# Keys of the first four tiles loaded in halves, idle products in any free PSUM bank, and a re-made order, in an attention and two-layer kernel on one core

## The chip, the core and the metric

The kernel runs on one core of a Trainium2 chip. Its engines work side by side, each through its own queue in order: TensorE (PE, with its weight loads, PEld), VectorE (DVE), ScalarE (ACT), GpSimd (POOL), and SyncE (SP), whose queue issues every DMA here. Times are microseconds. The metric is the device time of one launch: 1057.6 us, the median of 3 runs (1056.24 to 1058.17).

## The reference

Four batches of 768 positions with eight heads of 64 go through an attention of a narrow band with a few global keys, then through two feed-forward stages, one after the other:

```
scores = q @ k^T / 8 - slope[h] * dist ;  kept where key < n_global or 0 <= rel < n_local
a = softmax(scores) ;  x = a @ v                    # 3072 tokens x 512
h = x @ w_in  (512 x 2048) ;  x = (h * cos(h)) @ w_out
h = max(x @ w2_in, 0)      ;  out = (h * h) @ w2_out
```

Everything is float32. The kernel carries most numbers as a high and a low float16 part, so that a product becomes three float16 products.

## The kernel before, in words

There are 24 tiles of 128 positions (six in a batch). The first tile of each batch (F0 to F3 here, tiles 0, 6, 12 and 18) sees only its own keys; these four make the first block of 512 tokens, and the other twenty follow in blocks of four. A tile has two head groups of four heads, g0 and g1.

For the four first tiles `attend32` works in float32. `prepare32` loads the keys and queries (`kq`, 512 KB, two of them each 256 KB for tile 0) and the values (`vt`, 256 KB). `group32` then does for one head group: scores (PE L836, 4 matmuls), the bias by products with an identity (PE L918; it needs the tables that ACT writes in L590), the largest (DVE L925), the scaling of that (L908 on POOL or DVE, L906 on ACT), the exponentials with their sums (ACT L932, four of them), a diagonal of the sums' reciprocals (DVE L851, L854, L855), the turning and weighing by that diagonal (PE L866), a copy out of PSUM (`cast`, L538 on ACT or L540 on DVE), the values (PE L875), and the two parts of x (L538 or L540, then DVE L887, into `xy_107`). Tiles after the first of a batch go through `group`: scores L965, reduction L974, exponentials L982, parts `p` (cast L538/L540, low part L525 on DVE or POOL), a transposing DMA (L996), values L1006.

Weights come packed. `decoded` unpacks a pair: DMA `raw` (1 MB, L628), ACT L63, DVE L70; then a cast (L538 or L540) and a low part (L525). The first layer's products are L1149 (first half) and L1165 (second half). The first L1149 that reads all of `xy_107` can start once the last L887 of the four first tiles is done.

The order of all this is made when the kernel is built. Each piece has a due time, shifted by a table (`SHIFTS`, one entry per tile, group or weight), and `Plan.run` puts the pieces on the engines by due time, free buffers and durations that are written in the code; where a piece may run on two engines (a cast on ACT or DVE, a low part on DVE or POOL), `Plan.run` chooses. Every engine then executes its pieces in that order. `idle_products` looks for places where PE has a gap in the plan and puts products with a zero matrix there (L1789, each 128 x 512). SP's DMAs stand on eight semaphores in turn, so that the ninth DMA waits until the first has landed; the buffers named `ld` (nine of them) hold keys, values and weights in turn.

Of the kernel before, what the change touches and what calls it, by code (L numbers as in the profile page):

```python
# [67 lines left out]
def join(nc, f, t, r, n):  # L68
# [14 lines left out]
    ('A', 0, 0): -3.1,  # L83
    ('A', 0, 1): -3.1,
    ('A', 1, 0): -10.1,
# [12 lines left out]
    ('A', 15, 1): -0.3,  # L98
    ('A', 16, 0): 4.6,
    ('A', 2, 0): 0.7,  # L100
    ('A', 2, 1): -3.1,
    ('A', 21, 0): 2.9,
    ('A', 21, 1): -1.8,
    ('A', 23, 1): -6.5,
    ('A', 3, 0): 2.4,
    ('A', 3, 1): -3.1,
    ('A', 4, 1): -0.3,
    ('A', 5, 0): -15.0,
    ('A', 6, 0): -4.6,
    ('A', 7, 1): 1.3,  # L110
    ('A', 8, 0): -18.8,
# [5 lines left out]
    ('F', 2): -6.6,  # L117
    ('F', 3): -6.3,
    ('G', 2): -0.9,
    ('G', 3): 0.8,  # L120
    ('P', 0): 1.6,
    ('P', 1): 1.6,
    ('P', 10): 2.7,
    ('P', 11): -11.7,
    ('P', 12): 7.9,
    ('P', 13): 1.8,
    ('P', 15): 0.3,
    ('P', 19): 0.4,
# [3 lines left out]
    ('P', 23): -0.9,  # L132
    ('P', 3): 1.6,
    ('P', 5): -0.6,
    ('P', 7): 9.5,
    ('P', 8): 5.3,
    ('P', 9): -0.2,
    ('S', 0): -0.2,
    ('S', 1): -0.2,
    ('S', 2): -2.4,  # L140
    ('S', 3): -0.2,
    ('V', 0): -2.2,
    ('V', 2): 12.2,
    ('V', 4): 8.5,
    ('V', 5): -1.1,
    ('W', 0, 0): 1.6,
    ('W', 0, 3): -31.2,
    ('W', 0, 7): -0.5,
    ('W', 1, 0): -17.2,
# [5 lines left out]
    ('W', 1, 6): -0.3,  # L155
    ('W', 1, 7): -0.3,
    ('X', 10): 0.6,
# [12 lines left out]
    ('X', 23): 9.8,  # L170
    ('X', 4): 5.7,
    ('X', 6): -25.7,
    ('X', 8): -2.7,
    ('X', 9): -2.1,
}
EARLY = 30.0
EITHER = 10.0
BEGIN = 1.3
RATE = 320.0
ROUNDS = 1  # L180
SPIN_FROM = 0.9
SPIN_PART = 0.75
# [16 lines left out]
class Plan:  # L199
# [95 lines left out]
    def run(self):  # L295
# [64 lines left out]
        while done < len(work):  # L360
            moved = True
            while moved:
                moved = False
                for e in engines:
# [47 lines left out]
                    if e == "SP":  # L412
                        issue, xfer = way[1]
                        end_issue = now + issue
                        bus = max(bus, end_issue) + xfer
                        end = bus + 1.8
                        free_at[e] = end_issue
                    else:
                        end = free_at[e] = now + way[1]
                        if e == "ACT" and o.tab not in (None, table):  # L420
                            table, end = o.tab, end + 1.3
                            free_at[e] = end
                            self.switches += 1
                        if way[2]:
                            port_until, port_by = end, e
# [50 lines left out]
def fast_path(ctx, tc, kq, vt, w, n_raw, out, judge, ask):  # L476
# [337 lines left out]
    def prepare32(T):  # L814

        s = nominal(T, 0)
        f_s[T], v32[T] = f, vf = new("ld"), new("ld")
        cuts = ((0, 2), (2, 4)) if T == 0 else ((0, 4),)
        for n, (c0, c1) in enumerate(cuts):
            dma(s - 12, 512 / len(cuts), lambda c0=c0, c1=c1: nc.sync.dma_start(  # L820
                out=f4(f)[:, :, c0:c1], in_=kq[T][:, :, c0:c1]), **own(f, n == 0))
        dma(s - 6, 256, lambda: nc.sync.dma_start(out=at(vf)[:, 0:DM], in_=vt[T]), new=[vf])

    def group32(T, g):
# [15 lines left out]

        k = dict(part=reads) if T == g == 0 else dict(r=reads)
        plan.add((("PE", 0.65, False),), s, scores, new=ps, lag=0.3, **k)
# [910 lines left out]
    def idle_products(order):  # L1753

        out, last, before, busy, sums = {}, None, {}, {}, {}
        for o in order:
            for b in o.gets:
                before[b] = busy.get((b.pool, b.slot), 0.0)
            for b in o.bufs:
                if b.slot is not None:  # L1760
                    busy[b.pool, b.slot] = max(busy.get((b.pool, b.slot), 0.0), o.end)
        for o in order:
            if o.eng != "PE":
                continue
            if last is not None and o.start < SPIN_UNTIL and biased[7].end < o.start:
                gap = o.start - last.end
                open_y = [y for y in sums.values() if y[1].end <= last.end]
                if gap > SPIN_FROM:
                    own_b = [b for b in o.gets if b.pool in banks and b.writers[0] is o]
                    bank, begin = None, last.end  # L1770
                    if open_y:
                        bank = open_y[-1][0]
                    elif own_b:
                        bank, begin = own_b[0], max(begin, before[own_b[0]] + 0.3)
                    n = int(SPIN_PART * (o.start - begin) / 0.216)
                    if bank is not None and n > 0:
                        out[o] = bank, n, not open_y
            for y in (b for bs in y_all for b in bs if b in o.bufs):
                if o is y.writers[-1]:
                    sums.pop(y, None)  # L1780
                elif o is y.writers[0]:
                    sums[y] = y, o
            last = o
        return out

    def spin(bank, n, fresh):

        for _ in range(n):
            nc.tensor.matmul(  # L1789
                out=at(bank), lhsT=nought, rhs=bias.rearrange("p h c -> p (h c)")[:, 0:512], start=fresh, stop=fresh,  # L1790
                skip_group_check=True)
# [252 lines left out]
```

## Time and profile before

| | us |
|---|---|
| median of 3 runs | 1057.6 (1056.24 to 1058.17) |
| profiled execution | 1058.62 |
| its span, first to last instruction | 1056.9 |
| PE busy in the span | 1032.5 (98%) |
| DVE busy | 826.8 (78%) |
| ACT busy | 700.3 (66%) |
| POOL busy | 336.5 (32%) |

The share of a busy engine is an average over the whole span; what a stage costs is read from the stage. The views used below are the busy time by stretch, the waits of PE, and the instructions of each engine in order of time in the first 60 us. In a timeline row the first number is the start, the second the time until the last of its instructions ended, and the bracket says how long the engine was idle before and who released it.

### The profile page before, as it was taken

The numbers are of one execution on the slowest core, as the hardware profiler recorded it, in microseconds if no ns is written. First come the engines' busy times: TensorE is split into PE (matmuls) and PEld (weight loads), VectorE is DVE, ScalarE is ACT, GpSimd is POOL, SyncE is SP. The second block draws the span as 40 slices with busy tenths as digits, with TensorE's granted clock in tenths as the row PEclk, the third lists the DMA queues.
The fourth block names the chain that finished last, engine by engine and source line by source line (L and its number), as shares of the span: only waits on it lengthen the run. The fifth ranks groups of instructions, "written<-read, shape, count | busy, mean of one in ns | idle before, by whom it ended". The sixth has DMA issues, their size and how long they took to land.

```text
span 1056.9 us, 24666 instructions
## 1 busy us (share of the span) xinstructions
PE 1032.5 (98%) x9991; PEld 805.3 (76%) x9991; DVE 826.8 (78%) x1615; ACT 700.3 (66%) x1249; POOL 336.5 (32%) x263
## 2 busy tenths in 40 slices
PE   6799999999999999999999999999999999999997
PEld 5555455546888555688888888888888888888886
DVE  7988999998899889797989658748568577487363
ACT  6988888877786879695545467648357377276361
POOL 1445345432544324263234114203214024033020
PEclk9899999999999999999999999999999999999999
DMA  7789997989999999999999984424333344334201
GB/s 283 231 221 256 293 242 221 225 246 335 247 250 276 266 253 229 205 282 262 295 346 336 338 301 147 144 91 140 130 129 122 126 143 147 114 124 136 91 2 42
DMA packets 170422, 218.46 MB, mean 207 GB/s; under 512 B 120000, under 2 KB 120512, under 8 KB 168768
## 3 DMA queue, kind: packets, MB, share of 16 engines
q1 hardware_dynamic: 170304, 216.84, 69.1%
q8 instruction: 79, 1.29, 0.5%
q14 instruction: 39, 0.32, 0.1%
HBM read 150.47 MB, written 36.70 MB: 177 GB/s over the span
## 4 chain that ended last, share of the span: by engine, by line
PE 93%; DVE 4%; ACT 1%; DMA 1%; issue 1%; SPq 0%; POOL 0%; DVEq 0%
PE hps L1260 31%; PE ypps L1396 19%; PE ypps L1211 12%; PE ypps L1165 11%; PE hps L1149 11%; PE hps L965 3%; PE hps L1006 3%; PE hps L1396 2%; DVE e L974 1%; DMA ld<-kq 1%; DVE p L525 1%; PE hps L836 0%; PE hps L1595 0%; ACT e L932 0%; DVE ld L525 0%
## 5 line engine op out<-in xcount | busy, mean ns | idle before, releaser
L1260 PEld LDWEIGHTS <-ld 128*128 128x128 f16 x2592 | 253.1, 98 | 29.8 <-issue 0.2
L1260 PE MATMUL hps<-ys,ld 128*128 128x256 f16 x2064 | 239.6, 273 | 0.0
L1454 DVE TENSOR_TENSOR t<-hps,t 128x512 f32<-128x512 f32 x180 | 123.8, 688 | 64.3 <-PE hps L1260 62.3
L1149 PE MATMUL hps<-xy,w 128*128 128x512 f16 x576 | 132.9, 383 | 3.0 <-DVE xy L887 2.3
L1211 PE MATMUL ypps<-g,ld 128*128 128x256 f16 x1152 | 132.7, 273 | 0.0
L1165 PE MATMUL ypps<-g,ld 128*128 128x512 f16 x576 | 132.4, 379 | 0.0
L1211 PEld LDWEIGHTS <-ld 128*128 128x128 f16 x1152 | 112.0, 98 | 13.4 <-issue 0.2
L1149 PEld LDWEIGHTS <-w 128*128 128x128 f16 x576 | 55.1, 98 | 66.9 <-issue 5.7
L1165 PEld LDWEIGHTS <-ld 128*128 128x128 f16 x576 | 55.1, 98 | 63.9 <-DVE ld L525 0.3
L698 POOL TENSOR_TENSOR t<-t 128x256 f32<-128x256 f32 x26 | 24.2, 931 | 230.1 <-DVE x L698 230.0
L1451 ACT ACTIVATE t<-t 128x512 f32<-128x512 f32 x72 | 45.1, 627 | 62.3 <-DVE t L1454 62.0
L525 POOL TENSOR_TENSOR g<-t,g 128x512 f16<-128x512 f32 (+1 forms) x43 | 60.8, 1418 | 80.1 <-ACT g L538 53.6
L525 DVE TENSOR_TENSOR g<-t,g 128x512 f16<-128x512 f32 (+1 forms) x89 | 74.9, 848 | 4.8 <-ACT g L538 4.2
L1422 DVE SCALAR_TENSOR_TENSOR v<-ypps,v 128x256 f32<-128x256 f32 x77 | 30.3, 421 | 59.7 <-ACT v L1431 52.3
L982 ACT ACTIVATE e<-e,nm 128x256 f32<-128x256 f32 x160 | 67.6, 497 | 2.5 <-DVE nm L974 2.2
L974 DVE CUSTOM_DVE_ANT_0 e<-hps,bias 128x256 f32<-128x256 f32 (+1 forms) x160 | 56.9, 411 | 11.1 <-PE hps L965 10.7
L538 ACT ACTIVATE g<-t 128x512 f16<-128x512 f32 x71 | 44.0, 624 | 29.0 <-DVE t L1193 28.0
L1286 ACT ACTIVATE t<-t 128x512 f32<-128x512 f32 x96 | 60.3, 628 | 2.6
L1396 PEld LDWEIGHTS <-kq 128*128 128x128 f16 x540 | 52.8, 98 | 6.5 <-DVE kq L525 0.5
L1396 PEld LDWEIGHTS <-g 128*128 128x128 f16 x504 | 49.3, 98 | 5.7
L1396 PEld LDWEIGHTS <-xy 128*128 128x128 f16 x504 | 49.3, 98 | 5.7
L63 ACT ACTIVATE top<-raw 128x1024 f16<-128x1024 bf16 x32 | 43.4, 1357 | 7.2 <-DVE dec L70 6.3
(223 smaller groups left out, 2048.7 us busy)
## 6 DMA issues: line engine op xcount, KB each, us to landing
ld<-w SPq DMA_DIRECT2D x146, 512.0 KB, 4.3
raw<-w SPq DMA_DIRECT2D x32, 1024.0 KB, 6.3
w<-ld SPq DMA_DIRECT2D x44, 512.0 KB, 3.9
ld<-kq SPq DMA_DIRECT2D x23, 512.0 KB, 6.2
ld<-vt SPq DMA_DIRECT2D x27, 256.0 KB, 5.2
yd<-xy SPq DMA_DIRECT2D x6, 1024.0 KB, 6.1
xy<-yd SPq DMA_DIRECT2D x6, 1024.0 KB, 5.1
ld<-w SPq DMA_DIRECT2D x24, 256.0 KB, 3.2
```

The costliest lines, as they stand in the source:

```text
L525: op.emit = lambda: eng[op.eng].tensor_tensor(out=out_f(), in0=src_f(), in1=hi_f(), op=ALU.subtract)
L538: nc.scalar.activation(out=out(), in_=src(), func=ACTF.Copy)
L974: nc.vector.tensor_tensor_reduce(out=at(e)[:, x, c0:c1], in0=p[:, c0:c1], in1=bias[:, h, b0:b0 + c1 - c0], scale=-SCALE, scalar=at(nm)[:, ...
L982: nc.scalar.activation(out=at(e)[:, x, 0:W], in_=at(e)[:, x, 0:W], func=ACTF.Exp, bias=at(nm)[:, x:x + 1], scale=-1.0,)
L1149: nc.tensor.matmul(out=at(ps), lhsT=w_view(wt)[:, a, j % 2, k * 128:(k + 1) * 128], rhs=x_view(src)[:, c, k, :], start=(n == 0), stop=(n = ...
L1165: nc.tensor.matmul(out=at(y_ps[d]), lhsT=wv[:, a, d * 128:(d + 1) * 128], rhs=at(g)[:, c], start=(j == 0 and n == 0), stop=(j == NJ - 1 an ...
L1211: nc.tensor.matmul(out=at(y_ps[d])[:, 256 * n:256 * n + 256], lhsT=w_view(wt)[:, a, u, d * 128:(d + 1) * 128], rhs=at(g)[:, z, 256 * u:256 ...
L1260: nc.tensor.matmul(out=at(bank)[:, 256 * u:256 * u + 256], lhsT=wv(a, u, kk), rhs=sv(c, kk), start=(fresh and u == n == 0), stop=(last and ...
L1286: act(due, 512, lambda: nc.scalar.activation(out=at(t), in_=at(t), func=ACTF.Square), w=[t])
L1396: nc.tensor.matmul(out=at(bank)[:, 256 * half:256 * half + 256], lhsT=gv(home)[:, z, c0:c0 + 128], rhs=wv(a, u), start=(q == half == u == ...
L1451: act(due, 512, lambda: nc.scalar.activation(out=at(t), in_=at(ps), func=ACTF.Relu, scale=ROOT), **k)
L1454: dve(due, 0.7, lambda: nc.vector.tensor_tensor(out=at(t), in0=at(bank), in1=at(u), op=ALU.add), port=False, **k)
```

## The change

Keys and queries of all four first tiles now come in two DMAs of 256 KB each, one per head group (`cuts`), not only those of tile 0. The second half has a due time 4 us after the first, and the values one 8 us later than they had. `group32` of head group g0 now waits for the first half alone in every first tile. The low parts and casts themselves are the same.

`idle_products` had put its products into a bank of a running sum or into the bank that the next instruction would take; now, without a running sum, it takes the PSUM bank that is free longest. In the built program the products with zeros rise from 17 to 48. In the plan a DMA that is issued between 2 and 8 us lands 1.2 us later than it did (`CROWDED`), which changes no instruction by itself but the order. Some sixty entries of `SHIFTS` are new or have another number, and so the order differs on every engine.

```diff
 SHIFTS = {
     ('A', 0, 0): -3.1,
-    ('A', 0, 1): -3.1,
+    ('A', 0, 1): -1.7,
...
+CROWDED = 1.2
...
-                        end = bus + 1.8
+                        end = bus + 1.8 + (CROWDED if 2.0 < now < 8.0 else 0.0)
...
-        cuts = ((0, 2), (2, 4)) if T == 0 else ((0, 4),)
-        for n, (c0, c1) in enumerate(cuts):
-            dma(s - 12, 512 / len(cuts), lambda c0=c0, c1=c1: nc.sync.dma_start(
+        for n, (c0, c1) in enumerate(((0, 2), (2, 4))):
+            dma(s - 12 + 4 * n, 256, lambda c0=c0, c1=c1: nc.sync.dma_start(
                 out=f4(f)[:, :, c0:c1], in_=kq[T][:, :, c0:c1]), **own(f, n == 0))
-        dma(s - 6, 256, lambda: nc.sync.dma_start(out=at(vf)[:, 0:DM], in_=vt[T]), new=[vf])
+        dma(s + 2, 256, lambda: nc.sync.dma_start(out=at(vf)[:, 0:DM], in_=vt[T]), new=[vf])
...
-        k = dict(part=reads) if T == g == 0 else dict(r=reads)
+        k = dict(part=reads) if g == 0 else dict(r=reads)
...
-            if last is not None and o.start < SPIN_UNTIL and biased[7].end < o.start:
-                gap = o.start - last.end
+            if last is not None and o.start < SPIN_UNTIL and biased[7].end < o.start and o.start - last.end > SPIN_FROM:
                 open_y = [y for y in sums.values() if y[1].end <= last.end]
...
+                if open_y:
+                    bank, begin = at(open_y[-1][0]), last.end
+                else:
+                    owner = {(k, i): 0.0 for k in banks for i in range(banks[k])}
+                    for b, end in held.items():
+                        if b.users[0].start < o.start:
+                            owner[b.pool, b.slot] = max(owner[b.pool, b.slot], end)
+                    (k, i), free = min(owner.items(), key=lambda x: x[1])
+                    bank, begin = slots[k][i], max(last.end, free + 0.3)
+                n = int(SPIN_PART * (o.start - begin) / 0.216)
```

The DMAs of SP at the program's start stood so before: `ld_0_71` is F0's keys, `ld_2_73` F1's, `ld_5_76` and `ld_6_77` those of F2 and F3, `ld_4_75` the keys of tile 1.

```order
L820 DMA ld_0_71<-kq 128x2x256
L822 DMA ld_1_72<-vt 128x512
L820 DMA ld_2_73<-kq 128x1024
L822 DMA ld_3_74<-vt 128x512
L797 DMA ld_4_75<-kq 128x1024
L820 DMA ld_0_71<-kq 128x2x256
L820 DMA ld_5_76<-kq 128x1024
L820 DMA ld_6_77<-kq 128x1024
L799 DMA ld_7_78<-vt 128x512
L628 DMA raw_0_69<-w 128x2x2048
```

In the changed kernel (lines are 15 higher) they stand so; `ld_0_71`, `ld_1_72`, `ld_4_75` and `ld_5_76` are the keys of the first tiles, `ld_6_77` those of tile 1.

```order
L835 DMA ld_0_71<-kq 128x2x256
L835 DMA ld_1_72<-kq 128x2x256
L837 DMA ld_2_73<-vt 128x512
L837 DMA ld_3_74<-vt 128x512
L835 DMA ld_4_75<-kq 128x2x256
L835 DMA ld_5_76<-kq 128x2x256
L835 DMA ld_0_71<-kq 128x2x256
L835 DMA ld_1_72<-kq 128x2x256
L644 DMA raw_0_69<-w 128x2x2048
L835 DMA ld_4_75<-kq 128x2x256
L835 DMA ld_5_76<-kq 128x2x256
L644 DMA raw_1_70<-w 128x2x2048
```

F1's first half has moved from behind F0's values to the place right behind F0's first half; the keys of tile 1 have moved behind both packed weights.

On DVE, between the bias tables and the second score group, these rows stood before (the four L925 are the largest of F0's and F1's g0, `kq_0_84` and `kq_1_85` the parts of later keys, L855 makes F0's first diagonal):

```order
L925 TENSOR_REDUCE nm_1_93<-hps_3_142 128x2
L540 CAST kq_0_84<-ld_4_75 128x1024
L908 TENSOR_SCALAR nm_1_93<-nm_1_93 128x4
L540 CAST kq_1_85<-ld_0_71 128x512
L525 TENSOR_TENSOR kq_0_84<-ld_4_75,kq_0_84 128x1024
L851 TENSOR_SCALAR sm_0_96<-sm_0_96 128x4
L854 RECIPROCAL sm_0_96<-sm_0_96 128x4
L855 TENSOR_TENSOR t_0_120<-ident_196,sm_0_96 128x512
L925 TENSOR_REDUCE nm_2_94<-hps_0_139 128x2
```

Now these stand there:

```order
L940 TENSOR_REDUCE nm_1_93<-hps_3_142 128x2
L786 SCALAR_TENSOR_TENSOR v_0_87<-ld_2_73,v_0_87 128x8x64
L923 TENSOR_SCALAR nm_1_93<-nm_1_93 128x4
L866 TENSOR_SCALAR sm_0_96<-sm_0_96 128x4
L869 RECIPROCAL sm_0_96<-sm_0_96 128x4
L870 TENSOR_TENSOR t_0_120<-ident_196,sm_0_96 128x512
L556 CAST kq_0_84<-ld_0_71 128x512
L940 TENSOR_REDUCE nm_2_94<-hps_0_139 128x2
```

The cast and low part of tile 1's keys have left DVE, the other cast stands behind the diagonal, and the low part of `v_0_87` has come in. On PE, between the bias products of F0 and F1 and the second scores of F0, which stood next to each other, there are now nine products with zeros.

On ACT, ahead of the exponentials of F3 (L932 with `sm_2_98`), these rows stood before (`L982` are tile 1's exponentials; the two `e` buffers have four each):

```order
L538 ACTIVATE kq_2_86<-ld_2_73 128x1024
L538 ACTIVATE t_3_123<-ypps_1_144 128x512
L982 ACTIVATE e_0_100<-e_0_100,nm_2_94 128x256 x4
L982 ACTIVATE e_1_101<-e_1_101,nm_3_95 128x256 x4
L538 ACTIVATE xy_0_107<-ypps_2_145 128x2x128
L538 ACTIVATE p_1_103<-e_1_101 128x1024
L906 ACTIVATE nm_1_93<-nm_1_93 128x4
L63 ACTIVATE top_0_68<-raw_0_69 128x1024
L932 ACTIVATE e_0_100,sm_2_98<-hps_0_139,nm_0_92 128x128 x2
```

Now these stand there:

```order
L554 ACTIVATE kq_2_86<-ld_8_79 128x1024
L554 ACTIVATE t_2_122<-ypps_0_143 128x512
L784 ACTIVATE v_1_88<-ld_1_72 128x8x64
L554 ACTIVATE t_3_123<-ypps_1_144 128x512
L997 ACTIVATE e_0_100<-e_0_100,nm_2_94 128x256 x4
L997 ACTIVATE e_1_101<-e_1_101,nm_3_95 128x256 x4
L554 ACTIVATE p_0_102<-e_0_100 128x1024
L554 ACTIVATE p_1_103<-e_1_101 128x1024
L921 ACTIVATE nm_1_93<-nm_1_93 128x4
L554 ACTIVATE w1_0_112<-dec_1_111 128x1024
L63 ACTIVATE top_0_68<-raw_0_69 128x1024
L947 ACTIVATE e_0_100,sm_2_98<-hps_2_141,nm_0_92 128x128 x2
```

The casts of `p_0_102` and of the first weights `w1_0_112`, which DVE did before, and the high part `v_1_88` have come in on ACT; one cast of x has left.

## Rows read from the trace of the kernel before

**Rows 1.** The page: busy time, share and instructions of PE and the others.
```profile
PE 1032.5 (98%) x9991; PEld 805.3 (76%) x9991; DVE 826.8 (78%) x1615; ACT 700.3 (66%) x1249; POOL 336.5 (32%) x263
```
**Rows 2.** Busy time by stretch: stretch, length, engines, granted clock, DMA share, GB/s.
```profile
0.00:60.00 60.00, 43.87 (x371) 30.88 (x372) 49.05 (x126) 46.23 (x123) 16.95 (x31) 0.91 0.77 246
60.00:160.00 100.00, 100.00 (x935) 51.95 (x934) 88.03 (x177) 84.76 (x130) 48.02 (x27) 1.00 0.95 262
160.00:240.00 80.00, 79.07 (x672) 40.97 (x671) 78.10 (x136) 62.16 (x107) 36.09 (x23) 1.00 0.89 227
240.00:1000.00 760.00, 758.33 (x7550) 635.86 (x7549) 579.77 (x1115) 483.15 (x848) 228.57 (x176) 1.00 0.68 207
```
**Rows 3.** Waits of PE, first 60 us: for whom, total us, times, longest.
```profile
PE hps L836 <- DMA ld<-kq: 7.6, 2, 5.0
PE hps L965 <- ACT e L932: 3.9, 2, 3.4
```
**Rows 4.** Timeline of PE: start, us, line, what, [idle before <-releaser].
```profile
8.84 1.22 PE L836 MATMUL hps<-ld 64*128 64x128 f32 x8 [2.60 <-DMA ld<-kq]
9.99 1.04 PE L918 MATMUL hps<-bias,ident 128*128 128x192 bf16 x8
12.39 1.92 PE L836 MATMUL hps<-ld 64*128 64x128 f32 x8 [1.36 <-ACT e L932]
16.37 2.06 PE L866 MATMUL ypps<-t,e 128*128 128x128 f32 x8
18.21 1.86 PE L1789 MATMUL ypps<-bias,nought 128*128 128x512 bf16 x4
19.91 1.05 PE L866 MATMUL ypps<-t,e 128*128 128x128 f32 x8
50.48 4.22 PE L1149 MATMUL hps<-xy,w 128*128 128x512 f16 x11 [2.34 <-DVE xy L887]
```
**Rows 5.** DMAs issued at 2.10 and 2.73 us: KB each, us to landing.
```profile
ld<-vt SPq DMA_DIRECT2D x1, 256.0 KB, 3.5
...
ld<-kq SPq DMA_DIRECT2D x1, 512.0 KB, 6.1
```
**Rows 6.** Timeline of DVE.
```profile
5.18 0.55 DVE L584 SCALAR_TENSOR_TENSOR ys<-x,nf,ys 128x320 f32<-128x320 f32 x1
...
12.77 1.22 DVE L525 TENSOR_TENSOR kq<-ld,kq 128x1024 f16<-128x1024 f32 x1
...
15.27 0.69 DVE L855 TENSOR_TENSOR t<-ident,sm 128x512 f32<-128x512 bf16 x1
...
42.87 3.16 DVE L525 TENSOR_TENSOR w<-dec,w 128x1024 f16<-128x1024 f32 x1
...
48.12 1.97 DVE L70 SCALAR_TENSOR_TENSOR dec<-raw,top 128x1024 int32<-128x1024 int32 x1
```
**Rows 7.** Timeline of ACT.
```profile
6.18 2.97 ACT L590 ACTIVATE bias<-ys 128x320 bf16<-128x320 f32 x8
...
11.53 0.37 ACT L932 ACTIVATE e<-hps,nm 128x128 f32<-128x128 f32 x1 [1.43 <-POOL nm L908]
...
41.28 1.07 ACT L538 ACTIVATE w<-dec 128x1024 f16<-128x1024 f32 x1
...
44.20 0.60 ACT L538 ACTIVATE t<-ypps 128x512 f32<-128x512 f32 x1 [0.61 <-PE ypps L866]
```
**Rows 8.** Busy time from the exponentials of F0's g1 to those of F3.
```profile
17.43:38.33 20.90, 17.56 (x193) 13.74 (x193) 19.22 (x69) 19.53 (x59) 7.17 (x5) 0.97 0.74 269
```
**Rows 9.** Timeline of POOL.
```profile
42.43 2.52 POOL L525 TENSOR_TENSOR w<-dec,w 128x1024 f16<-128x1024 f32 x1 [4.33 <-ACT w L538]
46.88 2.13 POOL L525 TENSOR_TENSOR kq<-ld,kq 128x1024 f16<-128x1024 f32 x1 [1.93 <-ACT kq L538]
```
**Rows 10.** Timeline of PE in the first layer's products.
```profile
94.86 1.03 PE L1789 MATMUL ypps<-bias,nought 128*128 128x512 bf16 x4
```
**Rows 11.** Groups by line: busy us, mean ns, idle before.
```profile
L982 ACT ACT_TABLE_LOAD x24 | 30.8, 1283 | 1.7 <-DVE nm L974 1.3
```

More of the change, by code (lines that the diff above doesn't have):

```diff
@@ L99 @@
     ('A', 16, 0): 4.6,
+    ('A', 17, 0): -8.9,
     ('A', 2, 0): 0.7,
     ('A', 2, 1): -3.1,
-    ('A', 21, 0): 2.9,
+    ('A', 21, 0): 1.8,
     ('A', 21, 1): -1.8,
+    ('A', 22, 1): 7.9,
     ('A', 23, 1): -6.5,
@@ L109 @@
     ('A', 6, 0): -4.6,
+    ('A', 6, 1): -7.2,
+    ('A', 7, 0): -1.3,
     ('A', 7, 1): 1.3,
@@ L117 @@
     ('F', 2): -6.6,
-    ('F', 3): -6.3,
+    ('F', 3): -4.5,
     ('G', 2): -0.9,
@@ L121 @@
     ('P', 0): 1.6,
-    ('P', 1): 1.6,
-    ('P', 10): 2.7,
+    ('P', 1): 5.2,
+    ('P', 10): 17.3,
     ('P', 11): -11.7,
@@ L126 @@
     ('P', 13): 1.8,
+    ('P', 14): -0.7,
     ('P', 15): 0.3,
@@ L132 @@
     ('P', 23): -0.9,
[L133 to L136, printed above, removed]
+    ('P', 3): 3.3,
+    ('P', 4): 13.6,
+    ('P', 5): 13.0,
+    ('P', 6): 13.6,
+    ('P', 7): 23.1,
+    ('P', 8): 3.6,
     ('P', 9): -0.2,
-    ('S', 0): -0.2,
-    ('S', 1): -0.2,
+    ('S', 0): -0.1,
+    ('S', 1): 9.7,
     ('S', 2): -2.4,
     ('S', 3): -0.2,
-    ('V', 0): -2.2,
+    ('V', 0): 8.7,
+    ('V', 1): 6.6,
     ('V', 2): 12.2,
@@ L145 @@
     ('V', 5): -1.1,
-    ('W', 0, 0): 1.6,
-    ('W', 0, 3): -31.2,
-    ('W', 0, 7): -0.5,
+    ('V', 6): 0.4,
+    ('W', 0, 0): 2.8,
+    ('W', 0, 1): 11.4,
+    ('W', 0, 2): 16.9,
+    ('W', 0, 3): -30.0,
+    ('W', 0, 4): -1.9,
+    ('W', 0, 5): -4.8,
+    ('W', 0, 6): 1.2,
+    ('W', 0, 7): 0.7,
     ('W', 1, 0): -17.2,
@@ L155 @@
     ('W', 1, 6): -0.3,
-    ('W', 1, 7): -0.3,
+    ('W', 1, 7): -9.4,
     ('X', 10): 0.6,
@@ L170 @@
     ('X', 23): 9.8,
-    ('X', 4): 5.7,
+    ('X', 4): -0.5,
+    ('X', 5): 4.9,
     ('X', 6): -25.7,
     ('X', 8): -2.7,
-    ('X', 9): -2.1,
+    ('X', 9): 0.9,
 }
@@ L1753, in idle_products @@
     def idle_products(order):
-        out, last, before, busy, sums = {}, None, {}, {}, {}
+        out, last, held = {}, None, {}
         for o in order:
-            for b in o.gets:
-                before[b] = busy.get((b.pool, b.slot), 0.0)
             for b in o.bufs:
-                if b.slot is not None:
-                    busy[b.pool, b.slot] = max(busy.get((b.pool, b.slot), 0.0), o.end)
+                if b.pool in banks:
+                    held[b] = max(held.get(b, 0.0), o.end)
+        sums = {}
         for o in order:
@@ L1764, in idle_products @@
                 continue
-            if last is not None and o.start < SPIN_UNTIL and biased[7].end < o.start:
-                gap = o.start - last.end
+            if last is not None and o.start < SPIN_UNTIL and biased[7].end < o.start and o.start - last.end > SPIN_FROM:
                 open_y = [y for y in sums.values() if y[1].end <= last.end]
[L1768 to L1777, printed above, removed]
+                if open_y:
[8 more added lines that the diff above has]
+                n = int(SPIN_PART * (o.start - begin) / 0.216)
+                if n > 0:
+                    out[o] = bank, n, not open_y
             for y in (b for bs in y_all for b in bs if b in o.bufs):
@@ L1789, in spin @@
             nc.tensor.matmul(
-                out=at(bank), lhsT=nought, rhs=bias.rearrange("p h c -> p (h c)")[:, 0:512], start=fresh, stop=fresh,
+                out=bank, lhsT=nought, rhs=bias.rearrange("p h c -> p (h c)")[:, 0:512], start=fresh, stop=fresh,
                 skip_group_check=True)
```

## The prediction, as it was put on record

> **What bounds the kernel now.** First the page: PE is busy 98% of the span [rows 1], so the 24.4 us in which it is not (1056.9 less 1032.5) are all that a better order can give, beside products that PE need not do and its clock. Then the busy time by stretch, to see where they lie: 16.1 us in the first 60, none from 60 to 160, 0.9 from 160 to 240, 1.7 from there to 1000 [rows 2]; the rest, 5.7, is the end of the program, which the change leaves alone. From 60 us on PE works nearly without a pause, and its work there is the same in both kernels; so the time moves by when the first layer starts, by products with zeros that stand behind that, and by new pauses behind it. The waits of PE in the first 60 us [rows 3] and its timeline [rows 4] say what sets that start: keys that land late, banks that ACT holds, and at the last DVE, whose L887 lets the first L1149 go at 50.48. The timelines of DVE and ACT [rows 6, 7] show why these come when they do: both are nearly full from 17 to 38 us, DVE 19.2 and ACT 19.5 of 20.9 [rows 8].
>
> The clock is read from like instructions: the turning L866 of one group took 2.06 us at 16.37 and 1.05 at 19.91 [rows 4], the lower level (1.2 GHz) and the upper (2.4 GHz); PE had worked without a pause since 12.39.
>
> **The change part by part.** Times are those of the profiled execution.
>
> *1, keys in halves.* F1's scores waited until 8.84 for 512 KB [rows 4, 5]. Its first half now stands where F0's values stood, 256 KB issued at 2.10 that landed after 3.5, at 5.6. Behind the scores stand the bias products, at 9.99 before. They need six of ACT's eight tables, 0.37 us each (2.97 by 8); ACT had v ahead of them and began at 6.18 [rows 7], now it can begin when DVE is done, at 5.73 [rows 6]: 5.73 + 2.2 = 7.95. That is 2.0 earlier, and F0's exponentials, 1.5 behind the first bias product (11.53 less 9.99), start at 9.5. If the half lands as the 512 KB did, at 8.8, nothing is won here. Three DMAs are added on SP, which waits for landings anyway. Tile 1's keys move behind both packed weights; some 4.7 MB come up to and with them after 5.6, at 269 GB/s, a mean with pauses [rows 8], 17.5 us: they land by 23, just when ACT comes to their cast. I count nothing; each us later would be one on ACT.
>
> *2, DVE.* F0's diagonal was done at 15.96, three us after its exponentials, since DVE had two casts and a low part of 1.22 in between [rows 6]. Two of them have left and one stands behind: exponentials until 10.9, three small instructions of 1.1, done at 12.0.
>
> *3, PE between these.* Nine products with zeros now stand behind the bias products (1.04, until 9.0). Four took 1.86 us at the lower clock [rows 4], so nine take 4.2, until 13.2, though the bank for F0's second scores is free 0.86 behind the start of the exponentials (12.39 less 11.53), at 10.4: they hold PE 2.8 us. Scores (1.2) and bias (0.5) follow, and the turning starts at 14.9, not 16.37: 1.5 won at the lower clock. But PE then works without a pause from 7.95 on; if that lifts the clock by 13, scores, bias and turning take half, and the turning ends at 15.1 instead of 18.4: 3.3 won. If nothing was won in 1, the idle products cost 0.5 here. I take 2.0, near the slow case, between +0.5 and -3.3.
>
> The page "TensorE: Matmul & The Clock Gate" of the Trainium skill says in Part 1 that the array is throttled by default and that activity lifts it. The rows agree that PE began at the lower level and rose while it was busy; by that rule alone the step would be 3.3, and the sum 1.3 lower.
>
> *4, ACT up to F3's exponentials.* From 17.43 to 38.33 ACT was busy 19.5 of 20.9 us [rows 8], so what goes in front of F3's exponentials delays them. It gets the cast of tile 1's keys, of `p_0` and of `w1_0`, 1.07 each [rows 7], and `v_1`, about 0.6 as the copy of the same 512 columns: 3.8. It gives up two copies of 0.60 and one cast of x, about 0.4: 1.6. Of the 2.2 more, its 1.4 of idle time can take some; 0.8 stays on the path. Won up to here: 2.0 - 0.8 = 1.2. Of the new idle products 24 stand in PE's wait for F3's banks (3.9 us in all [rows 3]); at 1.03 for four [rows 10] they take at most 6.2 us, PE comes to them about 1.5 us earlier, and they end near the bank's release: nothing. If PE comes no earlier they cost up to 2.3. Six more stand in a wait for a copy on DVE, 1.6 us at that price, which DVE's list of work hides.
>
> *5, from there to the first L1149.* 50.48 - 38.33 = 12.15 us of the same pieces. PE has not been idle for 3.4 us before the turning of F3, so it is at the upper clock, and ACT's wait of 0.61 for that at 44.20 [rows 7] goes. DVE's low part of `w1_0` took 3.16 us [rows 6], from 42.87 until 1.1 us after POOL's own low part ended (42.43 + 2.52) [rows 9]: it stood behind POOL. The same happens at 48.12, 1.97 us for an unpacking, with POOL busy from 46.88 to 49.01. In the new order both pairs meet again in the same sequence, so nothing changes. Start of the first layer: 1.2 + 0.6 = 1.8 earlier, 48.7. What is late next is the same L887 on DVE behind the same L70.
>
> *6, idle products behind the start.* Four stood at 94.86 while PE had no pause around them [rows 2, 10]; they are gone, -0.9.
>
> *7, the rest.* By the two orders POOL has nine elementwise instructions fewer and DVE fourteen more, some 4.3 us by their shapes (0.3 to 0.7 each); ACT has six table loads more, 1.28 each [rows 11], 7.7 us, and five other instructions fewer. DVE has 12.0 us of idle time from 60 to 160 and ACT 15.2; from 160 to 240 DVE has 1.9 [rows 2]. The early part hides it, the stretch from 160 to 240 not all of it. PE's pauses behind 60 are 2.6 in all. I take +1.0, between -2.6 (all pauses go) and +6.9 (all of DVE's work and one pair of loads fall on PE).
>
> Sum: 1058.6 - 1.8 - 0.9 + 1.0 = 1056.9. The profiled execution was 1.0 above the median of the runs, so 1055.9. A measurement of this kernel tells about 0.2%, 2.1 us, from no change: below 1055.5 is faster, above 1059.7 slower.
>
> **The rivals.**
>
> *DVE comes before POOL.* In step 5 DVE reaches the low part of `w1_0` 4.5 us after F3's first exponential, POOL its own after 4.1. Now DVE waits only for the last exponentials (about 3.0) and its diagonal (1.1): 4.1, a tie. If DVE is first, its 3.16 become 1.22, and the unpacking behind it may also come before POOL, 1.97 becoming 1.22: 2.7 more, 1053.2. For it: the tie. Against it: POOL needs only one cast of ACT, and the trace has POOL first both times. The page "SBUF — State Buffer" of the Trainium skill says, in "SBUF: two separate sides", that DVE and GpSimd share a port pair as an exclusive lock, and that whichever starts first keeps it for the whole instruction. The trace agrees: DVE ended 1.1 us behind POOL, not in parallel with it.
>
> *The start stays.* The half lands late, or the nine idle products at the lower clock eat the gain and ACT's 0.8 the rest: start as before, the four idle products gone, pauses +1.0: 1057.7. For it: DVE and ACT are nearly full from 17 us on, and ACT's work there grows. Against it: the bias products depend on two landings that the trace shows early.
>
> *PE starves in the mixed stretch.* From 140 to 340 us each exponential of a tile needs a table load on ACT and a slot on DVE, which is 98% busy from 160 to 240 [rows 2]. If all of DVE's 4.3 us and half a pair of loads (1.3) reach PE, the rest costs +5.6 instead of +1.0: 1060.5, slower. It decides from 4.8 on, where the gains of 2.7 are eaten and 2.1 is added. For it: DVE has 1.9 us to spare there and takes over POOL's work. Against it: PE waited 0.9 us there in spite of that load, so the buffers between carry something.
>
> That the change does not do what it says would show as idle products that wait for their bank; PE's bank choice has none whose reader is still to come, so I give it no case of its own.
>
> **How the numbers follow.** Forecast 0.44, with 1053.9 to 1058.2 as its own range; of it 0.19 lies below 1055.5. DVE first 0.18, all faster. Start stays 0.18, all within. Starving 0.20, of which 0.01 within. Faster 0.37, same 0.44, slower 0.19. The range reaches down through most of the first rival, to 1052.2, and up to the middle of the last, 1060.5; about 0.09 is left out at either end.
>
> **What would show it.** Step 1: the bias products start near 8 us, and F1's scores before 6.5. Step 2: the first diagonal is done near 12. Step 3: nine products with zeros end near 13, and the next turning starts between 14 and 15; its duration tells the clock. Step 4: F3's exponentials start near 37.1, and PE's wait for them is gone. Step 5: DVE's low part takes 3.1 again (1.2: the first rival), the first full L1149 starts near 48.7. Step 6: no idle products behind 50. Step 7: PE's pauses between 60 and 1000 are near 3.6; above 7 it is the last rival. The forecast is wrong if the first layer starts at 50 or later, or below 47, or if the pauses behind it change by more than 3.

## The result, and the profile after

| | median, us | lowest to highest | runs |
|---|---|---|---|
| before | 1056.92 | 1054.95 to 1058.17 | 6 |
| changed | 1063.28 | 1062.52 to 1065.24 | 6 |

The ratio is 1.0068, with a 95% interval of 1.0056 to 1.0080: slower by 0.7%, 6.4 us, where 1055.9 was forecast with 1060.5 as the upper end. The profiled execution took 1064.6 with a span of 1062.8; that of before 1058.6 and 1056.9.

The page and the busy time by stretch, as in [rows 1, 2]:

```profile
PE 1038.3 (98%) x10019; PEld 806.2 (76%) x10022; DVE 827.8 (78%) x1629; ACT 706.3 (66%) x1250; POOL 324.9 (31%) x254
```

```profile
0.00:60.00 60.00, 50.91 (x464) 33.16 (x468) 50.20 (x132) 50.65 (x130) 19.89 (x34) 0.97 0.82 266
60.00:160.00 100.00, 100.00 (x906) 51.77 (x905) 91.51 (x185) 90.19 (x137) 39.59 (x24) 1.00 0.94 267
160.00:240.00 80.00, 78.50 (x671) 41.39 (x670) 74.25 (x128) 57.65 (x100) 32.47 (x19) 1.00 0.85 222
240.00:1000.00 760.00, 751.27 (x7458) 628.54 (x7456) 577.36 (x1119) 479.69 (x836) 226.16 (x171) 1.00 0.68 204
```

PE's share is 98% as before and tells nothing. The third and fourth row do: PE's pauses are 1.5 and 8.7 us, where they were 0.9 and 1.7 [rows 2]. The start went the other way. PE's timeline, to be laid beside [rows 4] (the lines of the kernel's functions have a number 15 higher than before, those of the casts and low parts one 16 higher):

```profile
8.13 2.88 PE L1804 MATMUL ypps<-bias,nought 128*128 128x512 bf16 x9
11.12 0.81 PE L851 MATMUL hps<-ld 64*128 64x128 f32 x8
12.09 1.14 PE L881 MATMUL ypps<-t,e 128*128 128x128 f32 x8
...
46.25 3.90 PE L1164 MATMUL hps<-xy,w 128*128 128x512 f16 x11 [2.29 <-DVE xy L902]
```

The turning (L881) starts at 12.09 instead of 16.37 and takes 1.14 instead of 2.06; the first full product (L1164) stands at 46.25 instead of 50.48. So 4.2 us were won there and lost again later. The timeline further on shows where; these are PE's pauses of more than 0.5 us from 60 to 1000:

```profile
178.35 0.89 PE L1021 MATMUL hps<-v,pt 128*128 128x65 f16 x24 [1.50 <-DVE nm L989]
292.75 4.34 PE L1226 MATMUL ypps<-g,ld 128*128 128x256 f16 x23 [3.90 <-DVE g L541]
323.87 2.67 PE L1226 MATMUL ypps<-g,ld 128*128 128x256 f16 x23 [0.91 <-DVE g L541]
407.74 0.32 PE L980 MATMUL hps<-kq 64*128 64x128 f16 x5 [0.69 <-DVE t L1208]
497.22 4.46 PE L1275 MATMUL hps<-ys,ld 128*128 128x256 f16 x24 [2.26 <-DMA ld<-w]
```

With three smaller ones they are 10.1, against 2.6 before. And the second row carries a cost of its own: the 23 products behind the long pause took 4.34, and the same 23 at 323.87 took 2.67. The granted clock of 290 to 300 us is 0.83: a part of it went at the lower level. The same follows the last pause: 24 products of L1275 take 4.46 there, 2.78 elsewhere (at 502.24, for one), and the granted clock of 495 to 505 us is 0.83 too.

By where PE reaches the same late product (L1411 near 655, L1396 before), the changed kernel is 6.4 behind (661.75 less 655.32). The account: start -4.2, the four idle products at 94.86 gone -1.0, pauses +7.5, lower clock behind two of them +1.7 and +1.7; that makes +5.7, and 0.7 stays without an owner. Of the 10.1 us of pauses, 6.3 stand at the first three, where PE waits for DVE, and 2.3 at the late load. From that product on the kernels need about as long, 401.1 us now and 401.6 before.

What made the longest pause? DVE's timeline up to it, and POOL's beside it:

```profile
278.44 0.68 DVE L541 TENSOR_TENSOR g<-t,g 128x512 f16<-128x512 f32 x1
279.19 0.69 DVE L556 CAST p<-e 128x1024 f16<-128x1024 f32 x1
...
287.55 2.62 DVE L556 CAST p<-e 128x1024 f16<-128x1024 f32 x1
290.09 2.60 DVE L541 TENSOR_TENSOR g<-t,g 128x512 f16<-128x512 f32 x1
```

```profile
287.38 2.25 POOL L541 TENSOR_TENSOR kq<-ld,kq 128x1024 f16<-128x1024 f32 x1 [4.10 <-DVE kq L556]
290.00 2.14 POOL L541 TENSOR_TENSOR p<-e,p 128x1024 f16<-128x1024 f32 x1 [0.38 <-ACT p L554]
```

The same two passes of DVE took 0.69 and 0.68 ten microseconds earlier, when POOL had no pass. Here each ends 0.5 us behind a pass of POOL that began just before it: 3.8 us lost in a row, and PE waits for the second. In the order POOL's pass on `kq` belongs behind DVE's two, but nothing ties it to them: it needs only the cast of `kq`, so it starts as soon as that ends. The pauses at 178 and 323 look alike (a cast of 2.34 for 0.42; two low parts in 3.23 for 1.3, each beside a 128x1024 pass of POOL):

```profile
175.27 2.34 DVE L556 CAST g<-t 128x512 f16<-128x512 f32 x1
319.98 3.23 DVE L541 TENSOR_TENSOR ld<-dec,ld 128x512 f16<-128x512 f32 x2
```

```profile
174.76 2.57 POOL L541 TENSOR_TENSOR kq<-ld,kq 128x1024 f16<-128x1024 f32 x1
320.35 2.31 POOL L541 TENSOR_TENSOR kq<-ld,kq 128x1024 f16<-128x1024 f32 x1 [2.40 <-ACT kq L554]
```

### The profile page after: what moved, and what is told of

It reads as the page before. It is cut to its first block, busy times and chain, and to the rows that moved or that the text cites. A ratio compares the mean times of both kernels' runs of the same rounds, so it can differ in the third digit from the quotient of the medians.

```text
span 1062.8 us, 24718 instructions
## 1 busy us (share of the span) xinstructions
PE 1038.3 (98%) x10019; PEld 806.2 (76%) x10022; DVE 827.8 (78%) x1629; ACT 706.3 (66%) x1250; POOL 324.9 (31%) x254
## 4 chain that ended last, share of the span: by engine, by line
PE 87%; DVE 8%; ACT 3%; DMA 1%; issue 1%; SPq 0%; POOL 0%; DVEq 0%; ACTq 0%
PE hps L1275 30%; PE ypps L1411 19%; PE ypps L1226 11%; PE hps L1164 10%; PE ypps L1180 10%; PE hps L980 3%; PE hps L1021 2%; PE hps L1411 2%; DVE e L989 1%; DVE ld L541 1%; DMA ld<-w 1%; DVE p L541 1%; DVE g L541 1%; ACT e L947 1%; DVE p L556 0%
## 5 line engine op out<-in xcount | busy, mean ns | idle before, releaser
L1275 PEld LDWEIGHTS <-ld 128*128 128x128 f16 x2592 | 254.0, 98 | 33.0 <-DMA ld<-w 2.5
L1275 PE MATMUL hps<-ys,ld 128*128 128x256 f16 x2064 | 240.9, 274 | 2.3 <-DMA ld<-w 2.3
L1226 PE MATMUL ypps<-g,ld 128*128 128x256 f16 x1152 | 135.2, 275 | 4.8 <-DVE g L541 4.8
L1164 PE MATMUL hps<-xy,w 128*128 128x512 f16 x576 | 132.6, 382 | 2.3 <-DVE xy L902 2.3
L1164 PEld LDWEIGHTS <-w 128*128 128x128 f16 x576 | 55.1, 98 | 65.9 <-issue 3.9
L541 POOL TENSOR_TENSOR g<-t,g 128x512 f16<-128x512 f32 (+1 forms) x37 | 51.0, 1380 | 101.6 <-ACT g L554 52.2
L541 DVE TENSOR_TENSOR g<-t,g 128x512 f16<-128x512 f32 (+1 forms) x95 | 72.8, 778 | 5.1 <-ACT g L554 4.6
L989 DVE CUSTOM_DVE_ANT_0 e<-hps,bias 128x256 f32<-128x256 f32 (+1 forms) x160 | 57.1, 412 | 13.5 <-PE hps L980 13.2
L1411 PEld LDWEIGHTS <-kq 128*128 128x128 f16 x540 | 52.7, 98 | 6.6 <-DVE kq L541 0.5
L1411 PEld LDWEIGHTS <-xy 128*128 128x128 f16 x504 | 49.3, 98 | 5.7
L1411 PEld LDWEIGHTS <-g 128*128 128x128 f16 x504 | 49.3, 98 | 5.7
L541 POOL TENSOR_TENSOR kq<-ld,kq 128x1024 f16<-128x1024 f32 (+1 forms) x17 | 37.6, 2211 | 35.9 <-ACT kq L554 17.6
```

Source lines behind the costliest of these rows:

```text
L541: op.emit = lambda: eng[op.eng].tensor_tensor(out=out_f(), in0=src_f(), in1=hi_f(), op=ALU.subtract)
L989: nc.vector.tensor_tensor_reduce(out=at(e)[:, x, c0:c1], in0=p[:, c0:c1], in1=bias[:, h, b0:b0 + c1 - c0], scale=-SCALE, scalar=at(nm)[:, ...
L1164: nc.tensor.matmul(out=at(ps), lhsT=w_view(wt)[:, a, j % 2, k * 128:(k + 1) * 128], rhs=x_view(src)[:, c, k, :], start=(n == 0), stop=(n = ...
L1226: nc.tensor.matmul(out=at(y_ps[d])[:, 256 * n:256 * n + 256], lhsT=w_view(wt)[:, a, u, d * 128:(d + 1) * 128], rhs=at(g)[:, z, 256 * u:256 ...
L1275: nc.tensor.matmul(out=at(bank)[:, 256 * u:256 * u + 256], lhsT=wv(a, u, kk), rhs=sv(c, kk), start=(fresh and u == n == 0), stop=(last and ...
L1411: nc.tensor.matmul(out=at(bank)[:, 256 * half:256 * half + 256], lhsT=gv(home)[:, z, c0:c0 + 128], rhs=wv(a, u), start=(q == half == u == ...
```

## The experiments

Times are medians; ratios are to the kernel before on the same chip, with a 95% interval. The edits are shown in short, and the remarks behind # were put in here.

**One pass moved.** The order is made and then one step of it is put on another engine; all else stands as it was.

```diff
     order = plan.order()
+    by = {o.n: o for o in order}
+    by[953].eng = "DVE"          # low part of kq, was POOL's at 287.38
```

> The changed kernel's order word for word, but one pass (the low parts of a tile's keys and queries, 128x1024, which GpSimd did from 287.38 to 289.63 us) stands on VectorE, behind the low part of g that PE waits for. Theory 1, the passes collide: PE's pause at 288.85 (3.90 us) is made by two VectorE passes that took 2.62 and 2.60 us, where 0.69 is usual, while GpSimd had its own pass; with GpSimd's pass gone they take 0.7 each, the pause falls below 0.6, the 23 products behind it take 2.6 instead of 4.34 because the clock is not let down, and the time is 4.5 to 5.6 lower, 1057.7 to 1058.8 against 1063.3. Theory 2, VectorE simply has too much work: it gets one pass of 1.13 us more, the pause stays at 3.9 or grows, or comes back further on, and the time is 1063 to 1064.5.

Measured: 1058.47 (12 runs), 1.0020 (1.0008 to 1.0033), 4.8 less than the changed kernel. DVE there:

```profile
285.80 0.69 DVE L556 CAST p<-e 128x1024 f16<-128x1024 f32 x1
286.40 0.69 DVE L541 TENSOR_TENSOR g<-t,g 128x512 f16<-128x512 f32 x1
287.00 1.22 DVE L541 TENSOR_TENSOR p<-e,p 128x1024 f16<-128x1024 f32 x1
288.13 0.69 DVE L1469 TENSOR_TENSOR t<-hps,t 128x512 f32<-128x512 f32 x1
288.74 2.73 DVE L541 TENSOR_TENSOR kq<-ld,kq 128x1024 f16<-128x1024 f32 x1
```

Both passes are back at 0.69, and PE's pause is gone; one of 0.81 stands at 293.15. DVE has more work and PE waits less: it was the collision, not the load. The moved pass itself collides (2.73 for 1.2), with POOL's `p`, and that is not free: DVE works without a pause from it to the reciprocals (L1037) that end PE's wait of 0.81, a wait which the changed kernel does not have. The sum fits the measured 4.8: 3.9 of pause and 1.7 of clock won, 0.8 lost.

**The pause filled.** 17 idle products stand in the 3.90 us.

```diff
+    turn = next(o for o in order if o.n == 1157)
+    idle[turn] = at(next(b for b in turn.bufs if b.pool == "yp")), 17, False
```

> The changed kernel, with 17 idle products of 128x512 (0.216 us each at the upper clock, 3.7 us) ahead of the 24 products in which PE's pause of 3.90 us stands. Nothing else is changed, so the wait itself stays. Theory 1, the pause also costs the clock behind it: the granted clock of 290 to 300 us goes from 0.83 to about 1.0, the 23 products take 2.6 instead of 4.34, and the time is 1.5 to 1.8 lower (1061.5 to 1061.8). Theory 2, the lower clock there is not the pause's doing, or its cost is hidden because VectorE is late anyway: 1063.0 to 1063.5. If the idle products themselves come late and reach past the wait, up to 0.5 is lost again.

Measured: 1061.13 (8 runs), 1.0038 (1.0024 to 1.0053), 2.2 less. PE at the place:

```profile
287.83 3.83 PE L1804 MATMUL ypps<-bias,nought 128*128 128x512 bf16 x17
291.50 0.27 PE L1226 MATMUL ypps<-g,ld 128*128 128x256 f16 x1
292.01 2.67 PE L1226 MATMUL ypps<-g,ld 128*128 128x256 f16 x23 [0.24 <-DVE g L541]
```

The wait is as long, the granted clock of 290 to 300 is 1.00, and the 23 products take 2.67. So the pause cost 3.9 and then 1.7 through the clock. The gain of 2.2 is 0.5 more than that, which the interval of about 1.5 us to either side covers.

**A load ahead in SP's queue.** The wait at 494.96 is for a load that was issued at 489.44 and landed 7.7 us later.

```diff
+    for n in (1752, 1637):       # the load of w; transposes of p
+        order.remove(by[n])
+        order.insert(order.index(by[1596]), by[n])
```

> The changed kernel with two issues of SP's queue moved ahead: the load of the weights that PE waits for at 494.96 us (2.26), and the transposes of the tile behind it, now stand in front of two transposes that wait for VectorE and of a load of 1 MB, instead of behind them. Theory 1, the load is late because of its place in the queue: issued near 484.6 instead of 489.4 it lands near 490; the pause goes, the 24 products behind it take 2.8 instead of 4.46, and the time is 3.0 to 4.0 lower (1059.3 to 1060.3). Theory 2, the queue is full there and only passes the lateness on: the transposes or the 1 MB load that were overtaken are late next, pauses of 2 us or more come between 485 and 520, and the time is within 1 of 1063.3.

Measured: 1065.95 (6 runs), 1.0085 (1.0067 to 1.0104): 2.7 more. The load is in time, and the 1 MB load that was overtaken is not:

```profile
498.59 1.35 ACT L63 ACTIVATE top<-raw 128x1024 f16<-128x1024 bf16 x1 [8.33 <-DMA raw<-w]
```

```profile
504.10 4.04 PE L1275 MATMUL hps<-ys,ld 128*128 128x256 f16 x24 [6.50 <-DVE t L1469]
```

ACT waits 8.3 for it (3.8 in the changed kernel), DVE's unpacking stands behind ACT, and the sums that free PE's banks stand behind that on DVE. The second theory held, at a higher price than it named.

**The raw load ahead as well.**

```diff
-    for n in (1752, 1637):
+    for n in (820, 1752, 1637):  # 820: the 1 MB load
```

> As the run with two issues moved ahead in SP's queue, but the 1 MB load of raw weights goes ahead with them, so that nothing which ScalarE, VectorE or PE wait for near 495 us is overtaken; two transposes and a store are what comes later. Theory 1, the 6.5 us pause of the run before came from the raw load (issued at 492.6 instead of 488.3: ScalarE waited 8.3 for it, VectorE 7.9 behind ScalarE, and the sums that free PE's banks stood behind them): with that load at 484.5, ScalarE's wait falls below 1, PE's pauses from 480 to 520 are below 1 in all, and the time is 2.5 to 4.0 under the changed kernel's (1059.3 to 1060.8). Theory 2, SP's queue is full from 470 to 500 us and some piece is late whatever the order: a pause of 2 us or more comes elsewhere from 480 to 540, and the time is within 1 of 1063.3.

Measured: 1062.54 (6 runs), 1.0056 (1.0038 to 1.0073), 0.7 less than the changed kernel. The 6.5 us pause is gone, which bears out what made it, but PE then waits 1.88 for the next load of weights. The second theory is nearer: the order in the queue decides which piece is late, not whether one is. What makes the loads land late there was not settled.

**Without the nine idle products.**

```diff
     idle = idle_products(order)
+    idle = {o: x for o, x in idle.items() if o.start > 12}
```

> The changed kernel without the nine idle products that PE runs from 8.13 to 11.0 us; the others stay. Theory 1, these products are what brings the clock up before the first turning products: those take 2.2 instead of 1.14, the second scores of the first tile 1.6 instead of 0.81, F3's exponentials start up to 1.5 later than 35.11, the first full product stands up to 1.5 later than 46.25, and the time is 0.7 to 1.5 higher. Theory 2, the halves of the keys and the order alone make the early start, and the chain of ScalarE and VectorE covers what PE loses: the first full product within 0.4 of 46.25, the time within 0.5 of the changed kernel's.

Measured: 1065.03 (6 runs), 1.0076 (1.0058 to 1.0095), 1.8 more. The first turning is back at the lower level:

```profile
10.82 1.32 PE L851 MATMUL hps<-ld 64*128 64x128 f32 x8 [2.34 <-DMA ld<-kq]
12.49 2.06 PE L881 MATMUL ypps<-t,e 128*128 128x128 f32 x8
...
48.33 2.53 PE L1164 MATMUL hps<-xy,w 128*128 128x512 f16 x11 [2.29 <-DVE xy L902]
```

The first theory held, a little above its range: the first full product is 2.1 later. The profiled starts of kernels that are alike up to there lie between 46.2 and 47.7, so the 2.1 is not sure to the microsecond, and neither is the 1.8: the single runs overlap (1063.99 to 1067.92, and 1062.52 to 1065.24 with the nine), and in this profile the load near 495 is waited for 1.5 longer. What is sure is the turning's 2.06 for 1.14.

**All three passes moved.**

```diff
-    by[953].eng = "DVE"
+    for n in (953, 542, 1204): by[n].eng = "DVE"
```

> As the run before with one pass moved, and two passes more of the same kind: in all three places where PE pauses for VectorE beside a 128x1024 pass of GpSimd (1.50 at 176.85, 3.90 at 288.85, 0.91 at 322.96 us), that pass stands on VectorE, behind what PE waits for. Theory 1, collisions at each place: the pauses of 1.50 and 0.9 fall below 0.4 too, and the time is another 1.5 to 2.4 below that of the one pass (1058.5), 1056.1 to 1057.0. Theory 2, VectorE is short of time and only the longest pause was a collision: the two others stay, or VectorE's 2.3 us more of work make new ones of 1 us or more behind 180 us: 1058 to 1060.

Measured: 1056.12 (12 runs), 0.9997 (0.9985 to 1.0010), 2.4 less than with one pass. The pauses at 178 and 323 are gone and no new one has come; PE's pauses from 60 to 1000 are 4.8. The first theory held, and the changed kernel is back at the time of before with three steps moved.

**Passes and queue together.**

```diff
+    for n in (953, 542, 1204): by[n].eng = "DVE"
+    for n in (820, 1752, 1637):
+        order.remove(by[n])
+        order.insert(order.index(by[1596]), by[n])
```

> Both edits in one: the three passes on VectorE, and the four issues of SP's queue in the new order. If the pauses are separate accidents of this order, the gains add: 1063.3 - 4.8 (measured for the first pass) - 1.5 to 2.4 - 2.5 to 4.0 = 1052 to 1054.5, which is 2 to 5 below the kernel before. If VectorE's work or the queue bounds the stretch, part comes back at other places and the time stays at 1056 or above.

Measured: 1056.41 (12 runs), 0.9995 (0.9982 to 1.0008). The gains did not add: the queue's edit gives nothing beside the passes. Single runs lie from 1053.1 to 1059.6, and the longer ones show a lower mean clock (0.995 against 0.998 to 1.000).

**The table of before in the new code**, the order made anew.

```diff
-SHIFTS = {                       # the table of the changed kernel
+SHIFTS = {                       # the table of the kernel before
```

> The changed kernel's code (keys in halves, the new rule for idle products, the later landings) with the table of numbers of the kernel before; the order is made anew from both. Theory 1, the halves and the idle products give the early start whatever the table: the first full product stands at 46 to 47 against 50.5 before. Theory 2, the table gives it: 48.5 or later. For the pauses behind 60 us: if the new table is what makes them, they fall to 2 to 4 in all and the time is 1053 to 1056; if any order that is made anew has some by chance, there are others at other places, 4 to 12 in all, and the time is 1056 to 1065.

Measured: 1065.39 (4 runs), 1.0081 (1.0061 to 1.0101). The first full product stands at 49.71: halves and idle products alone win only 0.8 at the start. The pauses are 7.6, at places of this order's own (here L526 is the low part, L541 the cast):

```profile
470.46 0.27 PE L1211 MATMUL ypps<-g,ld 128*128 128x256 f16 x1 [2.72 <-DVE g L541]
473.32 4.70 PE L1211 MATMUL ypps<-g,ld 128*128 128x256 f16 x23 [2.59 <-DVE g L526]
```

```profile
470.67 2.61 DVE L526 TENSOR_TENSOR g<-t,g 128x512 f16<-128x512 f32 x1
```

```profile
470.47 2.25 POOL L526 TENSOR_TENSOR ld<-dec,ld 128x1024 f16<-128x1024 f32 x1 [3.28 <-ACT ld L539]
```

It is the same picture at another place: POOL 0.2 us ahead, DVE's 0.69 becomes 2.61, and PE loses 2.6 and its clock.

**The new table in the old code**, the order made anew.

```diff
-SHIFTS = {                       # the table of the kernel before
+SHIFTS = {                       # the table of the changed kernel
```

> The code of the kernel before (keys whole but for the first tile's, values between them, the old rule for idle products, no later landings) with the new table of numbers; the order is made anew from both. Theory 1, the halves with the nine idle products and the table are needed together for the early start: the first full product at 48.5 to 51 us. Theory 2, the table alone gives it: 46 to 48. Behind 60 us both tables and codes seem to give chance pauses: 4 to 12 us in all at places of its own, some of them VectorE passes of 1.5 us or more beside a pass of GpSimd, and a time of 1058 to 1068. If the new table itself is what makes the pauses of the changed kernel, they stand at the same places (near 177, 289 and 495 us).

Measured: 1065.99 (4 runs), 1.0072 (1.0052 to 1.0092). First full product at 48.94; pauses of 10.1, the largest 2.69 at 401, none where the changed kernel has them. Ahead of the largest, four passes of DVE in a row, from 392.31 on, take 7.2 where 3.0 is usual, each behind a pass of POOL. The table alone does not give the early start either.

**Later landings left out**, the order made anew.

```diff
-CROWDED = 1.2
+CROWDED = 0.0
```

> The changed kernel with the planned landings of its first loads 1.2 us earlier (as the planner of the kernel before has them); nothing else is edited, but the order is made anew. Theory 1, the pauses behind 60 us are chance in any order that is made anew: an edit that touches the plan for 6 us at its start alone gives pauses at other places, between 3 and 14 us in all, and a time anywhere from 1055 to 1067. Theory 2, they belong to the table of numbers: the same pauses at the same places, 9 to 11 us in all, and 1062.5 to 1064.5.

Measured: 1061.31 (8 runs), 1.0043 (1.0027 to 1.0059). First full product at 47.64, pauses of 5.9 at 412, 466 and 493 to 503; the three DVE pauses of the changed kernel are not there. But this order puts 17 idle products at 133 to 138 us, 4.2 in all, into a stretch where PE had no pause. The first theory held for those: a change to six microseconds of the plan moves every pause for DVE. The wait for loads near 495 stays, shorter (1.01 and 1.15).

**Idle products in what is left**, on top of the three passes.

```diff
+    bank, _, fresh = idle[by[317]]          # ahead of the first full product
+    idle[by[317]] = bank, 16, fresh         # 6 before
+    idle[by[1758]] = at(next(b for b in by[1758].gets if b.pool == "h")), 8, True
```

> The run with three passes moved to VectorE, and idle products in the two longest pauses that are left: ten more (16 in all) ahead of the first full product near 46 us (pause 2.29), and eight ahead of the product that waits for its weights near 488 us (pause 2.19). No wait is changed. Theory 1, what makes this kernel's single runs lie between 1054.5 and 1058.8 is the clock, which falls behind these pauses in some runs and not in others (the 11 products behind the first took 3.90 in one run and 2.53 in another, the 24 behind the second 4.46 and 2.79): with the pauses filled the clock stays up in every run, the median falls by 1 to 2 to 1054.0 to 1055.2, and the runs lie closer together; that is 2 to 3 below the kernel before. Theory 2, the spread comes from the waits themselves (when the loads land), or the clock falls elsewhere: the median stays within 0.5 of 1056.1, the spread at some 4 us, and against the kernel before it is a draw again.

Measured: 1055.62 (11 runs), 0.9988 (0.9976 to 1.0000). Between the two theories: the load behind the filled pause was late instead, 2.72, and the 24 products behind that took 4.46.

**All of it**, the eight at the load that is late in this order: the edits of the passes, of the queue and of the idle products, with one number changed.

```diff
-    idle[by[1758]] = at(next(b for b in by[1758].gets if b.pool == "h")), 8, True
+    idle[by[1769]] = at(next(b for b in by[1769].gets if b.pool == "h")), 8, True
```

> The three passes on VectorE, the new order of the four issues in SP's queue, and idle products where that order leaves its two longest pauses: ten more ahead of the first full product near 46 us, eight ahead of the product that waits for its weights near 490 us (pause 1.83). In the run before, the eight stood ahead of a load that was then on time, and the next load was waited for 2.72 us with the clock falling behind it; here they stand at the load that is late in this order. Theory 1, the clock makes the spread of single runs: all runs within 1053 to 1056, median 1054.0 to 1055.0, 0.2 to 0.3% below the kernel before. Theory 2, the lateness of the loads moves from run to run whatever stands around it: median 1055.5 to 1056.5, spread 4 us.

Measured: 1054.65 (11 runs, 1053.9 to 1056.6), 0.9978 (0.9968 to 0.9987): faster than both kernels, by 2.2 and 8.6 us. The spread of single runs is 2.7 where it was 6.6 without the idle products, and their mean clock is 0.999 or 1.000 in every one; a part of that may belong to the hour of measuring, since the kernel before spread over 2.9 beside these runs and over 4.9 beside the others. PE at the load:

```profile
492.97 2.79 PE L1275 MATMUL hps<-ys,ld 128*128 128x256 f16 x24 [1.18 <-DMA ld<-w]
```

PE still waits, and the products behind the wait keep the upper clock.

## Why the prediction was wrong

Steps 1 to 5 had the mechanisms right and came out too cautious. Bias products: 7.28 (forecast 7.95). First diagonal: done at 11.78 (12.0). Nine idle products: ended at 11.0 (13.2), because the clock came up while they ran. That is the fast case of step 3, and more: the turning starts 4.3 and ends 5.2 earlier, where 2.0 was taken and 3.3 was the end. Leaving them out put the turning back to 2.06 us and the median 1.8 up; the scores behind them then start at 10.82 instead of 11.12, so they hold PE some 0.3 and not 2.8, and give it the clock. The page "TensorE: Matmul & The Clock Gate" of the Trainium skill, Part 1, says that activity releases a throttle which is there by default. The trace agrees, 1.14 instead of 2.06: the prediction named this and took a value near the slow case. Step 4: from the turning to F3's exponentials 23.0 instead of 22.0 us, +1.1 (forecast +0.8); they start at 35.11 (37.1). Step 5: DVE's low part of `w1_0` stood behind POOL again, 3.16 us, so the first rival did not come; the first full product stands at 46.25, which is below the 47 that the prediction named as its own refutation. Of the 4.2 us won there, the new code with the old table gives 0.8 and the new table in the old code 1.5; it takes both. Step 6 held: no idle products behind 50.

**Step 7 failed.** It took "+1.0" for "the rest" and the runs show +7.5 of pauses and +3.4 of lower clock, 10.9. Two things in its working were wrong. It priced the pauses as a sum of work: so many instructions more on DVE, so much idle time to hide them. But work was not what PE waited for; a pass more on DVE took 4.8 us off the time. The price is one of meetings between DVE and POOL. From 60 to 660 us, DVE's low parts and casts from SBUF lost some 38 us to passes that took over 0.3 longer than the same shape undisturbed (45 passes and 37.7 before, 35 and 37.9 after). The total did not change; which of them PE stands behind did. The prediction used that rule twice at 43 and 48 us and never for the rest of the program. And it took the pauses of before, 2.6, as the base to which work is added, with nothing for the clock behind a pause. Four orders made anew (the changed kernel's, the old table, the new table, the landings) have 10.1, 7.6, 10.1 and 5.9: 2.6 is the lowest of the five, each read from one profile, and nothing of it is handed on to an order made anew. Not all of the 10.1 is meetings: the wait for the late load is 2.3 of it, with 1.7 of the clock, and what makes that load late stays open.

The page "SBUF — State Buffer" of the Trainium skill, section "SBUF: two separate sides", calls DVE's and GpSimd's common port pair an exclusive lock, kept by whoever starts first for the whole instruction. The trace agrees, in both kernels: each held pass ends behind a pass of POOL by a time that goes by its own shape, 0.28, 0.55 or 1.08 us where it takes 0.42, 0.69 or 1.21 undisturbed. So nearly all of it runs after POOL's pass, not beside it.

The last rival, "PE starves in the mixed stretch", had the right sign and place (pauses above 7 were its stated sign) and the wrong cause: it too counted work and table loads. Its price, +5.6, was half of what came, and the lower clock was in neither. The range missed because its upper end was drawn through the middle of that rival.

Open stay the 0.7 of the account, and what makes the loads of weights late near 490 us.

## What to carry to other kernels

Where an order is made by a planner and run by engines that each keep only their own sequence, a small change at the start deals all meetings behind it anew: price it by what one bad meeting costs (here 1 to 4 us, and in some 1.7 more for the clock) and by how many other orders have, not by the work that moved. When such an order comes out slower, look for the two or three places where PE waits, see which pass there took several times its usual length, and move the other engine's pass that stood beside it. A pause that can't be removed can be filled: idle products took the clock's share of it away.

## What the runs showed that was not expected

- A pause of PE of about 2 us is followed by the lower clock in some executions and not in others: 24 products behind a wait of 2.17 took 4.46 in one kernel, behind 2.19 in another 2.79. One of 3.90 cost 1.3 to 1.7 in each of the profiles that has it.
- The clock rose while PE ran nine products with zeros at 8.13: they took 2.88, at the lower level nine would take 4.2 (four took 1.86 [rows 4]); PE had worked since 4.80 without a pause.
- In SP's queue an issue moved some 5 us ahead made the time 2.7 worse, since a 1 MB load that it overtook was issued 4.3 later and ACT, DVE and PE each wait in sequence.
